# Where the weight conversion of the expert next but one stands among full and half slots, in attention with a mixture of experts

## The chip, the cores and the metric

One core of a Trainium2 chip runs the whole program. The metric is the device time of one execution in microseconds (us), and the time of a kernel is the median of its runs. A separate profiled execution gives the trace, on which all positions in time below ("at 395.56") are counted from the start of its span.

## What is computed

An attention step over 4 x 8 x 576 rows of 64 gives x, 2304 tokens of 512 numbers. Each token then goes to the one expert of eight with the largest logit, and is scaled by its softmax value:

```
logits = x @ w_gate                       # 2304 x 8
expert_idx = argmax(logits, axis=1)
gate_w = softmax(logits)[arange(N), expert_idx]
for e in range(8):
    xe = x[expert_idx == e]
    h = maximum(xe @ w1[e], 0.0)          # 512 -> 1024
    out[expert_idx == e] = gate_w[...] * (h @ w2[e])   # 1024 -> 512
```

Everything is float32 outside. How many tokens an expert has is known only on the chip, so the loops over the experts run on counts that are read from memory there.

## The kernel before

**Slots.** Attention and routing take the first 262 us or so; what follows is the experts. The kernel takes them in the order 1, 2, ... 7, 0, one position e = 0 to 7 after another ("the fourth expert" is e = 3). The tokens of an expert are cut into slots: full ones of 128 tokens, and behind them at most one half slot, for a rest of at most 64 tokens. A slot runs like this:

- GpSimd gathers the rows of 128 tokens for a later slot (L1489, with the copy of the indices in L1538) and scatters finished rows (L1504).
- VectorE splits the gathered rows into two f16 parts, `xn` (L1780, L1783).
- SP issues two transposing DMAs of `xn` into `xB` (`xtrans`, L1411). SP's queue also issues the weight loads (`load`, L1384), and takes both in program order.
- VectorE copies `xB` to `xT` (L1794), once both transposes have landed and TensorE no longer reads the old `xT`.
- TensorE runs the first product (`first_part`, L1582: 96 matmuls, 5.52 us in a full slot), VectorE applies the relu and splits the result (L1751, L1753), and TensorE runs the second product (`second_part`, L1598 in full and L1595 in half slots). ScalarE moves the result out (L1711 in full slots).

So the body of a slot on VectorE (`dve_body`, L1772) is: `xn` for the *next* slot, the two relus of this one, `xT` for the next one, and at the end the register loads for the next expert's counts (L1303).

**Weights.** The matmuls are f16, on weights that have been split into a high part (`conv_hi`, ScalarE, L1272) and a low part (`conv_lo`, VectorE, L1276). An expert's weights are eight units of 128 x 1024; four units are a "state". State i is a half of the weights of position 1 + i // 2, so the states 2e and 2e + 1 belong to the expert that follows e, and 2e + 2 and 2e + 3 to the one next but one. Loaded units lie in one of two staging buffers by the position's parity (`m_stage` or `mem` in the trace), converted ones in one of three (`m_w` and two named `mem`).

**Which slot converts what** is set by counters, on ScalarE and VectorE alike (`conv_loops`, L1319). For each e, whatever of `now` (2e, 2e + 1) is missing is converted in a first slot. Then `full(nxt)` (L1356) gives the full slots one state each of `nxt` (2e + 2, 2e + 3); and if there is a half slot, `last(nxt)` (L1365) looks whether a state of `nxt` is still missing, and converts it there. All these cases are written out one behind another in the program, and the counts choose among them by branches; so much of the code is jumped over.

**What SP loads when** follows a counter `ld` of the states loaded (L1430 to L1480). `turn(i)` stands for a slot that converts state i, `rest()` for a slot that converts nothing; each first issues the slot's transposes (`slot()`) and then loads one state ahead. A state's loads are four DMAs of 512 KB, and wait where the staging buffer is still to be converted.

The cut of the conversions in a slot's body (`K["cuts"]`, L1789) puts the four `conv_lo` of a full slot around the relus, one, one, and two behind the copy of `xT`; in a half slot all four stand behind that copy.

Of the kernel before, what the change touches and what calls it, by code (L numbers as in the profile page):

```python
# [1224 lines left out]
def experts(nc, tc, es, x_dram, mem, rout, w1, w2, out):  # L1225
# [16 lines left out]
    PE, A, V, G, SP = nc.tensor, nc.scalar, nc.vector, nc.gpsimd, nc.sync  # L1242
# [12 lines left out]
    with tc.tile_critical():  # L1255
# [63 lines left out]
        def conv_loops(eng, rr, body):  # L1319
# [11 lines left out]
            for e in range(NE):  # L1331
# [33 lines left out]
                def last(states):  # L1365
                    if states:
                        with eng.If(eng.snap(c) < states[0] + 1):
                            step(e, 1, states[:1])
                        with eng.Else():
                            last(states[1:])  # L1370
                    else:
                        step(e, 1)

                full(nxt)
                if nxt:
                    with eng.If(more[1]()):
                        last(nxt)
                else:
                    with eng.While(more[1]):
                        step(e, 1)  # L1380
# [7 lines left out]
        r2 = SP.alloc_register("m_sp_r2")  # L1388
        SP.reg_mov(r2, 2)
        splim = [SP.alloc_register(f"m_sp_lim{i}") for i in range(2)]  # L1390
        nt = {}
        for n in "hl":
            nt[n] = SP.alloc_register(f"m_sp_{n}")
# [33 lines left out]
        SP.wait_ge(S["cn"], 7)  # L1427
        SP.reg_mov(splim[1], 1)
        SP.reg_load(splim[0], cnt[0:1, 0, 1:2])
        for e in range(NE):  # L1430
            now, nxt = ([i for i in range(2 * e + k, 2 * e + k + 2) if c0 <= i < 14] for k in (0, 2))

            def more(r=r1):
                return SP.snap(r) < SP.snap(splim[e % 2])

            def slot():
                xtrans()
                if e + 1 < NE:
                    SP.reg_load(splim[(e + 1) % 2], cnt[0:1, e + 1, 1:2])

            def load_next(j):
                loads(j)
                SP.reg_mov(ld, j + 1)

            def turn(i):
                slot()
                if i == c0:
                    SP.wait_ge(S["sc0"], 16)
                    SP.sem_inc(S["ya"], 1)
                SP.reg_add(cr, cr, 1)  # L1450
                with SP.If(SP.snap(ld) < i + 1):
                    load_next(i)
                with SP.If(SP.snap(ld) < i + 2):
                    load_next(i + 1)
                with SP.Else():
                    load_next(i + 2)

            def rest():
                slot()
                if 2 * e + 5 < 14:  # L1460
                    with SP.If(SP.snap(ld) < 2 * e + 6):
                        load_next(2 * e + 5)

            def turns(states):
                if states:
                    with SP.If(more()):
                        turn(states[0])
                        turns(states[1:])
                else:
                    with SP.While(more):  # L1470
                        rest()

            if now:
                with SP.If(SP.snap(cr) < 2 * e + 2):
                    if len(now) == 2:
                        with SP.If(SP.snap(cr) < 2 * e + 1):
                            with SP.If(more(r2)):
                                turn(now[0])
                            with SP.Else():
                                turn(now[0])  # L1480
                                SP.reg_add(cr, cr, 1)
                    with SP.If(SP.snap(cr) < 2 * e + 2):
                        turn(now[-1])
            turns(nxt)
        for n in "hl":
            spw("tx" + n, nt[n])

# [354 lines left out]
```

## Time and profile before

| | us |
|---|---|
| median of 3 runs | 498.99 (498.46 to 499.39) |
| the profiled execution | 493.86 |
| its span in the trace | 492.1 |
| TensorE busy | 459.1 |
| VectorE busy | 355.0 |
| ScalarE busy | 221.3 |
| GpSimd busy | 213.4 |

The span is what the trace covers; the profiled execution lasted 1.8 us longer than that, and stands 5.1 us below the median of the runs. "Issue" in the rows is time in which an engine waited for nothing that the profile shows. A row of a timeline gives the start, the busy time, the engine, the line, what is written from what, the shape, the number of instructions in the row, and in brackets the idle time ahead of it with what ended it. PE is TensorE, DVE is VectorE, ACT is ScalarE, POOL is GpSimd; SPq is the time in which SP issues DMAs.

In this run the slots by position are: e = 0 three full ones (and one taken ahead of the loops), e = 1 one full, e = 2 seven full, e = 3 one half, e = 4 five full and a half, e = 5 one half, e = 6 a full and a half, e = 7 one half.

### The profile page before, as it was taken

Reading aid. Unit: us, or ns where it says so; the run is one execution under the profiler, and the core shown is the slowest. Engines: PE = TensorE matmul, PEld = TensorE weight load, DVE = VectorE, ACT = ScalarE, POOL = GpSimd, SP = SyncE. Lnnn points to the kernel's source line nnn. Section 1 sums busy time; section 2 is a strip of 40 time slices with the busy share of each in tenths; the row PEclk is TensorE's granted clock in tenths of the full one; section 3 lists DMA queues with packets and bytes.
Section 4 is the critical chain, followed back from the end, with each engine's and each line's share of the span. In section 5 each row is a group of like instructions: output and inputs, shape, how many; then the busy total and the mean of one; then the engine's idle time right before and its main releaser. Section 6 shows DMA issues by size and latency. Waiting matters only on the chain.

```text
span 492.1 us, 14309 instructions
## 1 busy us (share of the span) xinstructions
PE 459.1 (93%) x5279; PEld 314.1 (64%) x5280; DVE 355.0 (72%) x785; ACT 221.3 (45%) x361; POOL 213.4 (43%) x396
## 2 busy tenths in 40 slices
PE   2999899999999989999978999999999989999885
PEld 1555456666666646657656777676677767777864
DVE  2788489786869647989885778788843489844682
ACT  3788565556666655457610444433300163300701
POOL 6567657367748344656331423132232122232132
PEclk9999799999999999999989999999999999999999
DMA  5667979999899989885247999799973199963232
GB/s 119 137 119 158 182 158 172 174 193 228 175 161 164 272 164 191 183 177 209 65 135 286 253 332 254 231 261 305 274 182 98 45 256 304 318 139 90 57 73 69
DMA packets 170106, 90.57 MB, mean 184 GB/s; under 512 B 151471, under 2 KB 152751, under 8 KB 170032
## 3 DMA queue, kind: packets, MB, share of 16 engines
q1 hardware_dynamic: 166192, 77.95, 67.8%
q0 software_dynamic: 3840, 11.80, 7.8%
q8 instruction: 26, 0.43, 0.3%
q14 instruction: 48, 0.39, 0.3%
HBM read 55.35 MB, written 11.60 MB: 136 GB/s over the span
## 4 chain that ended last, share of the span: by engine, by line
PE 64%; DVE 12%; SPq 8%; DMA 6%; issue 5%; ACT 2%; POOL 1%; DVEq 1%; POOLq 0%; ACTq 0%
PE m_ph L1582 18%; PE m_py L1598 16%; PE o L565 7%; PE st L491 5%; SPq L275 3%; PE loc L677 3%; PE sm L596 3%; PE sn L404 2%; SPq L277 2%; DMA m_xB<-m_xn 2%; DMA QT<-mem 1%; DVE mem L1276 1%; PE wm L882 1%; DVE m_w L1276 1%; PE sn L421 1%
## 5 line engine op out<-in xcount | busy, mean ns | idle before, releaser
L1582 PEld LDWEIGHTS m_ph<-m_xT,mem 128*128 128x128 f16 x1344 | 66.0, 98 | 5.9 <-issue 3.3
L1582 PE MATMUL m_ph<-m_xT,mem 128*128 128x128 f16 (+1 forms) x1344 | 67.1, 212 | 2.6 <-DVE m_xT L1794 2.6
L1711 ACT ACTIVATE m_y<-m_py 128x512 f32<-128x512 f32 x17 | 10.2, 597 | 121.6 <-PE m_py L1598 121.6
L510 ACT ACTIVATE aT<-st 128x512 f32<-128x512 f32 x96 | 55.2, 594 | 17.6 <-PE st L491 17.1
L412 DVE TENSOR_REDUCE mt<-sn 128x1 f32<-128x512 f32 (+4 forms) x83 | 54.2, 663 | 12.2 <-PE sn L410 10.0
L495 POOL TENSOR_SCALAR_AFFINE_SELECT aT<-aT 128x128 f32<-128x128 f32 (+2 forms) x160 | 48.0, 317 | 31.9 <-ACT aT L510 29.9
L1598 PE MATMUL m_py<-mem,m_hT 128*128 128x512 f16 x264 | 58.9, 379 | 1.8 <-DVE m_hT L1751 1.8
L565 PE MATMUL o<-aT,mem 128*64 128x320 f32 (+4 forms) x320 | 59.2, 433 | 0.0
L1751 DVE TENSOR_SCALAR m_hT<-m_ph 128x512 f16<-128x512 f32 (+1 forms) x46 | 29.0, 631 | 38.5 <-PE m_ph L1582 37.3
L1538 POOL COPY m_ig<-r_idx 128x1 int32 x22 | 4.0, 184 | 112.9 <-DVE m_xn L1783 111.8
L491 PE MATMUL st<-mem 128*128 128x64 f16 (+6 forms) x224 | 46.8, 262 | 0.4 <-ACT aL L532 0.2
L1598 PEld LDWEIGHTS m_py<-mem,m_hT 128*128 128x128 f16 x264 | 25.3, 98 | 30.3 <-issue 2.0
L491 PEld LDWEIGHTS <-mem 128*128 128x128 f16 (+1 forms) x448 | 32.9, 99 | 16.3 <-issue 4.4
L1582 PEld LDWEIGHTS m_ph<-m_xT,m_w 128*128 128x128 f16 x768 | 40.9, 98 | 3.1 <-issue 1.1
L491 PE MATMUL st<-QT,mem 66*128 66x64 f16 (+6 forms) x224 | 42.3, 262 | 0.4 <-ACT QT L455 0.4
L1582 PE MATMUL m_ph<-m_xT,m_w 128*128 128x128 f16 (+1 forms) x768 | 41.8, 216 | 0.9 <-issue 0.7
L1598 PE MATMUL m_py<-m_w,m_hT 128*128 128x512 f16 x168 | 37.4, 379 | 0.0
L565 PEld LDWEIGHTS o<-aT,mem 128*64 128x64 f32 x320 | 25.3, 137 | 16.7 <-issue 9.8
L1504 POOL DMA_INDIRECT out_dram<-m_y,m_is x23 | 27.2, 1184 | 19.9 <-POOL m_is L1510 19.9
L404 PE MATMUL sn<-mem 128*128 128x128 f16 (+3 forms) x158 | 31.2, 275 | 1.5 <-DVE mt L412 1.1
L1490 POOL DMA_INDIRECT m_xg<-x_scratch,m_ig x22 | 24.0, 1089 | 17.5 <-POOL m_ig L1538 17.5
L1753 DVE SCALAR_TENSOR_TENSOR m_hT<-m_ph,m_hT 128x512 f16<-128x512 f32 (+1 forms) x46 | 29.1, 633 | 1.6
(259 smaller groups left out, 904.2 us busy)
## 6 DMA issues: line engine op xcount, KB each, us to landing
mem<-in_moe_w_dram SPq DMA_DIRECT2D x40, 512.0 KB, 6.1
m_stage<-in_moe_w_dram SPq DMA_DIRECT2D x24, 512.0 KB, 6.6
mem<-in_k_dram SPq DMA_DIRECT2D x32, 128.0 KB, 3.0
mem<-in_q_dram SPq DMA_DIRECT2D x32, 128.0 KB, 2.8
mem<-in_v_dram SPq DMA_DIRECT2D x32, 128.0 KB, 2.8
x_scratch<-xb SPq DMA_DIRECT2D x3, 1152.0 KB, 5.9
mem<-mem SPq DMA_DIRECT2D x6, 288.0 KB, 4.1
x_scratch<-xb SPq DMA_DIRECT2D x1, 864.0 KB, 3.8
```

The lines of the kernel that those rows point to most:

```text
L404: nc.tensor.matmul(ps[:, c:c + k1 - k0], QT[:, 5 * hh + t, :], keys(hh)[:, k0:k1], start=(c == 0), stop=(k1 == parts[-1][3] and hh == part ...
L412: nc.vector.reduce_max(out, v, axis=AX.X)
L491: nc.tensor.matmul(ps[:, c:c + n], kk[:, kb, :], qq[:, w:w + n], start=(first and i == 0 and j == 0), stop=(last and i == 1 and j == len(p ...
L495: nc.gpsimd.affine_select(out=ap, in_=ap, pattern=pattern, compare_op=ALU.is_ge, fill=0.0, base=base, channel_multiplier=-1)
L510: nc.scalar.activation(out=a, in_=ps, func=AF.Exp, scale=ESC)
L565: nc.tensor.matmul(o[64 * hh:64 * hh + 64, q0:q0 + n], vv, aa, start=(j == 0), stop=(j == 4), skip_group_check=True)
L1490: G.indirect_dma_start(out=x.rearrange("p h e -> p (h e)"), out_offset=None, in_=x_dram, in_offset=bass.IndirectOffsetOnAxis(ap=i, axis=0) ...
L1504: G.indirect_dma_start(out=out, out_offset=bass.IndirectOffsetOnAxis(ap=i, axis=0), in_=ysb[:, j], in_offset=None, bounds_check=bound, oob ...
L1582: mm = PE.matmul(ph[i2][:, f, 0:N], w[:, kc, c:c + 128], x[:, j, kc, 0:N], start=(i == 0), stop=(i == 11), skip_group_check=True)
L1598: mm = PE.matmul(py, hh, ww[:, 4 + ff // 2, c:c + 512], start=st, stop=sp_)
L1751: V.tensor_scalar(out=hT[i2][0][:, :, 0:N], in0=ph[i2][:, :, 0:N], scalar1=0.0, scalar2=None, op0=ALU.max).then_inc(S[hi], 1)
L1753: V.scalar_tensor_tensor(out=hT[i2][1][:, :, 0:N], in0=ph[i2][:, :, 0:N], scalar=0.0, in1=hT[i2][0][:, :, 0:N], op0=ALU.max, op1=ALU.subtr ...
```

## The change

On ScalarE and VectorE, `last` is given no states for e up to 4: a half slot of these experts converts nothing of the expert next but one. For e = 5 (the sixth position; later ones have no `nxt`) it is as before. On SP, `turns` follows: for e up to 4 only full slots make a `turn`, by a count of full slots that SP now loads for each expert (`spful`), and the half slot is a `rest()`. `rest()` now loads the states 2e + 4 and 2e + 5, whichever are not yet loaded, where it loaded 2e + 5 alone; and `turn` asks before it loads state i + 2. The new lines shift the numbers behind them by 2 to 10.

```diff
@@ -1374,7 +1374,7 @@
                 full(nxt)
                 if nxt:
                     with eng.If(more[1]()):
-                        last(nxt)
+                        last(nxt if e > 4 else [])
                 else:
                     with eng.While(more[1]):
                         step(e, 1)
@@ -1388,6 +1388,8 @@
         r2 = SP.alloc_register("m_sp_r2")
         SP.reg_mov(r2, 2)
         splim = [SP.alloc_register(f"m_sp_lim{i}") for i in range(2)]
+        spful = [SP.alloc_register(f"m_sp_ful{i}") for i in range(2)]
+        SP.reg_mov(spful[1], 1)
         nt = {}
         for n in "hl":
             nt[n] = SP.alloc_register(f"m_sp_{n}")
@@ -1427,6 +1429,7 @@
         SP.wait_ge(S["cn"], 7)
         SP.reg_mov(splim[1], 1)
         SP.reg_load(splim[0], cnt[0:1, 0, 1:2])
+        SP.reg_load(spful[0], cnt[0:1, 0, 0:1])
         for e in range(NE):
             now, nxt = ([i for i in range(2 * e + k, 2 * e + k + 2) if c0 <= i < 14] for k in (0, 2))
 
@@ -1437,6 +1440,8 @@
                 xtrans()
                 if e + 1 < NE:
                     SP.reg_load(splim[(e + 1) % 2], cnt[0:1, e + 1, 1:2])
+                    if e + 1 < 5:
+                        SP.reg_load(spful[(e + 1) % 2], cnt[0:1, e + 1, 0:1])
 
             def load_next(j):
                 loads(j)
@@ -1453,17 +1458,19 @@
                 with SP.If(SP.snap(ld) < i + 2):
                     load_next(i + 1)
                 with SP.Else():
-                    load_next(i + 2)
+                    with SP.If(SP.snap(ld) < i + 3):
+                        load_next(i + 2)
 
             def rest():
                 slot()
-                if 2 * e + 5 < 14:
-                    with SP.If(SP.snap(ld) < 2 * e + 6):
-                        load_next(2 * e + 5)
+                for j in (2 * e + 4, 2 * e + 5):
+                    if j < 14:
+                        with SP.If(SP.snap(ld) < j + 1):
+                            load_next(j)
 
             def turns(states):
                 if states:
-                    with SP.If(more()):
+                    with SP.If(more() if e > 4 else SP.snap(r1) < SP.snap(spful[e % 2])):
                         turn(states[0])
                         turns(states[1:])
                 else:
@@ -1482,6 +1489,9 @@
                     with SP.If(SP.snap(cr) < 2 * e + 2):
                         turn(now[-1])
             turns(nxt)
+            if nxt and e < 5:
+                with SP.If(more()):
+                    rest()
         for n in "hl":
             spw("tx" + n, nt[n])
 
```

VectorE at the end of the half slot of e = 3, before: behind the copy of `xT` come four conversions (`m_w_4100` is a converted unit, `mem_61` a staged one), then the counts and the jump to the next expert.

```order
L1753 SCALAR_TENSOR_TENSOR m_hT_4112<-m_ph_4123,m_hT_4111 128x4x64
L1794 COPY m_xT<-m_xB 128x1024
L1276 SCALAR_TENSOR_TENSOR m_w_4100<-mem_61,m_w_4100 128x1024 x4
L1303 TENSOR_LOAD r_cnt x2
L1310 ISA
L1367 UNCONDITIONAL_BRANCH
```

The same place after:

```order
L1763 SCALAR_TENSOR_TENSOR m_hT_4112<-m_ph_4123,m_hT_4111 128x4x64
L1804 COPY m_xT<-m_xB 128x1024
L1303 TENSOR_LOAD r_cnt x2
L1310 ISA
L1376 UNCONDITIONAL_BRANCH
L1335 COMPARE_AND_BRANCH
```

The conversions are gone from this branch; the copy is followed by the counts.

SP in the half slot of e = 3, before (`m_stage_4113` takes the units of states 10 and 11, `mem_61` those of 8 and 9): behind the two transposes stand three loads of a state under branches, of which the counter lets one run.

```order
L1411 DMA_TRANSPOSE m_xB<-m_xn_4106 128x4x128
L1439 TENSOR_LOAD r_cnt
L1450 ISA
L1451 COMPARE_AND_BRANCH
L1384 DMA mem_61<-in_moe_w_dram 128x1024 x4
L1451 UNCONDITIONAL_BRANCH
L1453 COMPARE_AND_BRANCH
L1384 DMA mem_61<-in_moe_w_dram 128x2x512 x4
L1453 UNCONDITIONAL_BRANCH
L1384 DMA m_stage_4113<-in_moe_w_dram 128x1024 x4
```

The same slot after:

```order
L1413 DMA_TRANSPOSE m_xB<-m_xn_4106 128x4x128
L1442 TENSOR_LOAD r_cnt
L1444 TENSOR_LOAD r_cnt
L1468 COMPARE_AND_BRANCH
L1384 DMA m_stage_4113<-in_moe_w_dram 128x1024 x4
L1468 UNCONDITIONAL_BRANCH
L1468 COMPARE_AND_BRANCH
L1384 DMA m_stage_4113<-in_moe_w_dram 128x2x512 x4
L1468 UNCONDITIONAL_BRANCH
```

Here the loads of states 10 and 11 stand one behind the other, each under its own branch, and a second register load has come in.

## Rows read from the trace of the kernel before

**Rows 1.** The page, busy time of each engine, share of the span, instructions.
```profile
PE 459.1 (93%) x5279; PEld 314.1 (64%) x5280; DVE 355.0 (72%) x785; ACT 221.3 (45%) x361; POOL 213.4 (43%) x396
```

**Rows 2.** Timeline, ScalarE: start, busy, line, out<-in, [idle before <-releaser].
```profile
392.90 3.90 ACT L1272 ACTIVATE m_w<-mem 128x1024 f16<-128x1024 f32 x4 [3.31 <-issue]
```

**Rows 3.** Timeline, VectorE, around the fourth expert's half slot (e = 3).
```profile
389.54 0.49 DVE L1780 TENSOR_SCALAR m_xn<-m_xg 128x512 f16<-128x512 f32 x1 [4.10 <-issue]
...
394.77 0.64 DVE L1794 COPY m_xT<-m_xB 128x1024 f16<-128x1024 f16 x1 [2.23 <-DMA m_xB<-m_xn]
395.33 4.61 DVE L1276 SCALAR_TENSOR_TENSOR m_w<-mem,m_w 128x1024 f16<-128x1024 f32 x4
399.87 0.47 DVE L1780 TENSOR_SCALAR m_xn<-m_xg 128x512 f16<-128x512 f32 x1
...
401.12 0.68 DVE L1751 TENSOR_SCALAR m_hT<-m_ph 128x512 f16<-128x512 f32 x1
```

**Rows 4.** Timeline, TensorE, first two full slots of e = 4.
```profile
395.56 5.52 PE L1582 MATMUL m_ph<-m_xT,mem 128*128 128x128 f16 x96 [1.09 <-DVE m_xT L1794]
...
401.95 5.34 PE L1598 MATMUL m_py<-mem,m_hT 128*128 128x512 f16 x24 [0.87 <-DVE m_hT L1751]
407.13 5.52 PE L1582 MATMUL m_ph<-m_xT,mem 128*128 128x128 f16 x96
...
417.67 5.52 PE L1582 MATMUL m_ph<-m_xT,mem 128*128 128x128 f16 x96
```

**Rows 5.** Chain of waits: start, length, what; ahead of fourth and sixth expert.
```profile
386.74 2.39 issue
...
454.35 0.14 issue
```

**Rows 6.** Timelines of VectorE and TensorE, into the sixth expert (e = 5).
```profile
453.09 0.42 DVE L1794 COPY m_xT<-m_xB 128x1024 f16<-128x1024 f16 x1
...
454.90 0.49 DVE L1780 TENSOR_SCALAR m_xn<-m_xg 128x512 f16<-128x512 f32 x1 [1.39 <-issue]
...
461.72 0.43 DVE L1794 COPY m_xT<-m_xB 128x1024 f16<-128x1024 f16 x1 [2.81 <-DMA m_xB<-m_xn]
...
462.29 5.52 PE L1582 MATMUL m_ph<-m_xT,mem 128*128 128x128 f16 x96 [1.16 <-DVE m_xT L1794]
```

**Rows 7.** Timeline of SP's DMA queue: start of issue, time issuing, line, DMAs.
```profile
260.31 4.03 SPq L1384 DMA_DIRECT2D mem<-in_moe_w_dram  x8
...
390.23 2.57 SPq L1411 DMA_TRANSPOSE m_xB<-m_xn  x2
394.26 2.41 SPq L1384 DMA_DIRECT2D m_stage<-in_moe_w_dram  x4
400.56 2.64 SPq L1411 DMA_TRANSPOSE m_xB<-m_xn  x2
404.56 1.95 SPq L1384 DMA_DIRECT2D m_stage<-in_moe_w_dram  x4
409.34 2.61 SPq L1411 DMA_TRANSPOSE m_xB<-m_xn  x2
```

**Rows 8.** DMA traffic in 40 equal slices: 260 to 278, then 404 to 416 us.
```profile
GB/s 0 0 46 200 328 400 337 382 391 377 308 363 366 397 428 391 432 378 406 413 388 381 410 364 373 387 401 387 387 396 354 275 102 22 101 343 437 0 0 0
...
GB/s 239 61 169 384 258 41 130 273 369 314 328 205 116 246 225 212 348 362 342 300 355 396 396 410 403 437 370 379 329 223 155 58 164 365 161 15 68 352 307 423
```

**Rows 9.** Timeline, VectorE: the copy for the slot from 417.67.
```profile
415.74 0.43 DVE L1794 COPY m_xT<-m_xB 128x1024 f16<-128x1024 f16 x1 [0.51 <-DMA m_xB<-m_xn]
```

**Rows 10.** Stretches: us, busy PE PEld DVE ACT POOL, granted clock, DMA share, GB/s.
```profile
261.30:268.30 7.00, 7.00 (x98) 5.70 (x96) 3.60 (x7) 0.00 (x0) 1.51 (x3) 1.00 0.99 366
405.60:413.40 7.80, 7.80 (x109) 6.48 (x108) 7.48 (x10) 4.50 (x5) 1.66 (x3) 1.00 1.04 295
251.40:254.70 3.30, 1.20 (x16) 0.79 (x15) 3.21 (x15) 0.84 (x2) 1.30 (x3) 1.00 0.50 171
254.80:258.10 3.30, 3.30 (x27) 2.09 (x26) 2.21 (x12) 0.80 (x4) 0.00 (x0) 0.50 0.43 112
```

## The prediction

> **What bounds the kernel now.** I read the page first: TensorE is busy for 459.1 us, 93% of the span [rows 1], so an edit counts only where TensorE stands idle, or where it would come to stand. The edit acts on slots with at most 64 tokens. The trace shows the order of the slots by the moving columns of L1582: after seven full slots comes one half slot (the fourth expert, e = 3), then five full slots and a half slot (e = 4), a half slot (e = 5), a full and a half slot (e = 6) and a half slot (e = 7); the first three experts have no half slot. In before, the half slot of e = 3 converts four units (ACT L1272, 3.90 us; VectorE L1276, 4.61 us for four) [rows 2, 3], the half slot of e = 4 converts nothing because everything up to state 11 is done by then, and that of e = 5 is the one the edit exempts. So in this run the edit acts in one place: state 8 goes from the half slot of e = 3 to the first full slot of e = 4, and states 9, 10 and 11 each go one full slot later.
>
> So I read the timeline around 395 us. TensorE ends the half slot, waits 1.09 us for VectorE's copy of xT, runs L1582 of the first full slot of e = 4 at 395.56, waits 0.87 us for VectorE's L1751, and starts the second full slot at 407.13 [rows 4]. From 395.56 to 407.13 are 11.57 us; the next slot takes 10.54 us, from 407.13 to 417.67 [rows 4]. VectorE shows why: its four L1276 occupy 395.33 to 399.94, and only behind them come the xn of the next slot (399.87) and the L1751 for which TensorE waits (401.12) [rows 3]. The first wait is another matter: xT is copied at 394.77, when the transposes have landed, and these start behind the xn of 389.54, ahead of which VectorE stood 4.10 us in "issue" [rows 3]. The chain of waits puts 2.39 us of it behind a single branch, at 386.74 [rows 5].
>
> **The change, part by part.**
>
> *Removed from the half slot:* four L1276, 4.61 us of VectorE, and four L1272 on ACT. Without them xn follows its xT copy as at the end of the next half slot, where no conversion stands between: copy 453.09, xn 454.90 [rows 6], 1.81 us. So xn comes at 394.77 + 1.81 = 396.6 instead of 399.87, the L1751 is ready when L1582 is, and the slot takes 10.54 instead of 11.57 us: **-1.03 us**. The wait of 1.09 us stays, as nothing in front of 389.54 gets shorter on that path.
>
> *Added to the four full slots of e = 4:* one conversion each in slots one to four instead of one to three. That costs nothing: the slot from 407.13 holds a conversion on both engines and takes 10.54 us [rows 4]. The cover is TensorE's own time; four L1276 are 4.61 us of it.
>
> *Moved on SP, the term that decides.* The queue of SP issues both the weight loads and the transposes that xT waits for, in program order. In before the half slot of e = 3 issues four loads at 394.26 (state 10), then come the next slot's transposes at 400.56, and state 11's four loads only behind these, at 404.56 [rows 7]. In after, rest() issues the loads of states 10 and 11 together in the half slot: eight DMAs of 512 KB, and the next slot's transposes stand behind all eight. Issuing eight took 4.03 us at 260.31 [rows 7], so SP is free at 394.26 + 4.03 = 398.3, early enough for transposes that in before start at 400.56. But the data are not there: in the stretch that begins with the eight loads of 260.31 the traffic stays between 300 and 432 GB/s until the slice at 273.95 and falls to 102 and 22 GB/s behind it, at 274.4 [rows 8], 14.1 us after the first issue. The same from 394.26 gives 408.4 for the drain.
>
> Do the transposes pass the loads? Two rows say no. With four loads issued at 404.56, the transposes are issued at 409.34 [rows 7]; the loads drain at about 413.3 (40 slices of 0.3 us from 404: 223, 155, 58 GB/s in the 30th to 32nd) [rows 8], and xT is copied at 415.74, after a DMA wait of 0.51 us [rows 9], 2.4 us after the drain and 6.4 us after the issue. With no load in flight the same transposes went from issue at 390.23 to the copy at 394.77 in 4.54 us [rows 3, 7]. So xT of the second full slot is copied at 408.4 + 2.4 = 410.8, and TensorE starts 395.56 - 394.77 = 0.8 us later, at 411.6, instead of 407.13: **+4.5 us**, the first gain already inside. The bounds: the loads, one gather (128 rows of 2304 B) and half a scatter are about 4.6 MB; at the 366 and 295 GB/s of two stretches full of loads [rows 10], counted from about 395.3, they drain at 407.9 and 410.9, and with 1.5 to 2.4 us to the copy TensorE starts at 410.2 to 414.1: +3.1 to +7.0 us. I take 4.5, since the stretch at 260 us is the same eight loads.
>
> The Trainium skill speaks to this as well: "DMA: Bandwidth & Descriptors", section "Queues, rings and completion order", has each DMA engine consume the descriptors of one issuing queue in ring order, which is against this change, and the row at 415.74 agrees. Its section "Specifications" gives 435 GB/s as the ceiling; by that alone 4.6 MB would drain in an estimated 10.6 us, TensorE would start near 409.1, and the term would be +2.0; the 295 to 366 GB/s of this trace decide.
>
> *TensorE's clock.* TensorE then stands idle from 395.56 + 10.54 = 406.1 to 411.6, 5.5 us, longer than the idle rows of TensorE quoted here (1.16 us at most) [rows 6]. After sparse work the granted clock has fallen to 0.50, the 1.2 GHz level: with TensorE busy for 1.20 of 3.30 us ahead of it, the stretch 254.80 to 258.10 ran at 0.50 [rows 10]. At half the clock 3.4 us of stretch do 1.7 us of work. I take one such stretch, **+1.7 us**, between 0 (it falls and recovers while TensorE is idle) and 3.4 (two of them).
>
> *The rest costs nothing.* SP's extra register load per slot falls into its wait for xn: xn starts at 399.87, and SP issues the transposes only at 400.56 [rows 3, 7]; uncovered it would be an estimated few tenths of a us per slot, since the whole time from the end of that xn at 400.34 to the issue is 0.22 us. States 12 and 13 are loaded in the third and fourth full slot of e = 4, one later than before; the conversion of state 12 stands in the half slot of e = 5, behind the copy at 461.72 [rows 6], some 30 us later. They meet the transposes as the loads at 404.56 do, and these delayed no matmul: xT copied at 415.74, next slot at 417.67.
>
> **Sum:** 4.5 + 1.7 = +6.2 us. The profiled execution lasted 493.86 us, and this sum would make it 500.1; the median of the runs is 498.99, 5.1 us above it, and I add the difference to the median: **505.2 us**.
>
> **The rivals.**
>
> *A code fetch falls on the chain of the sixth expert.* VectorE's program is shorter by the conversions of five experts. The chain shows the same jump over untaken code twice: at 386.74, ahead of the fourth expert, it waits 2.39 us, and at 454.35, ahead of the sixth, 0.14 us [rows 5]. The second stands directly ahead of the xn at 454.90, from which transposes and the copy at 461.72 follow, for which TensorE waits 1.16 us [rows 6]; there a wait of 2.39 instead of 0.14 passes on in full: +2.25, 507.5 us. For it: which pair waits can only depend on where the code lies, and all code behind the first expert moves. Against: in before one of the two waits. The mirror case, that the wait at 386.74 goes and none comes, moves everything behind 389.54 forward by 2.25: 503.0 us. The Trainium skill has the mechanism in "Runtime: NRT & Kernel Launch", section "Instruction fetch mechanics": a taken branch that leaves the two pages at hand waits for a DMA fetch; no row here shows pages.
>
> *The transposes are not held up.* Then the slot starts when TensorE is free, at 406.1, the clock stays up, and what is left is -1.03 us: 498.0. This decides itself at one point: xT must be copied by 405.3, so transposes must land some 5 us ahead of the 410.8 above. For it: transposes have been issued while loads were in flight in most slots, and in them TensorE ran on. Against: those had four loads ahead of them, not eight, and were issued 5 us behind the loads; and 4.6 MB by 404 would be over 500 GB/s, more than any stretch of [rows 8] or [rows 10].
>
> *The change does not do what it says,* because the slots are other ones than I read: time as before, 499.0.
>
> **How the numbers follow.** Transposes behind eight loads: 0.50, 502.0 to 509.4 (3.1 + 0 to 7.0 + 3.4 us); with the fetch at the sixth expert 0.28, at 507.5; with the wait at 386.74 gone 0.07, at 503.0; transposes not held 0.11, at 498.0, about two thirds of it beyond 0.2% (1.0 us, about what a measurement of this kernel can tell from no change); no effect 0.04. Slower 0.85, same 0.07, faster 0.08. The range 502.0 to 509.4 leaves out the last two and the upper end of the fetch case.
>
> **What would show it.** In the profile after: no L1276 between the xT copy near 394.8 and the next xn; eight L1384 in a row on SP ahead of a transpose; VectorE's copy of the following xT with a DMA wait of 4 us or more; a TensorE idle of some 5.5 us ahead of the second full slot of e = 4, and a stretch of clock 0.50 behind it; at the sixth expert an "issue" wait of over 2 us, or none. I am wrong if that copy waits under 1 us, and wrong in size if the traffic drains before 407 or the clock stays at 1.00.

## The result and the profile after

| | before | after |
|---|---|---|
| median of 16 runs each, us | 498.5 (495.14 to 502.3) | 504.85 (500.14 to 509.2) |
| ratio, 95% interval | | 1.012 (1.009 to 1.0149) |
| profiled execution, us | 493.86 | 504.78 |
| stretch of the experts in that trace, us | 226.34 | 235.02 |

The change makes the kernel slower, by 6.35 us between the medians and by 6.0 us (interval 4.5 to 7.4 us) by the ratio; 6.2 were forecast. Medians and ranges here and below are over all runs, while the ratios leave out single runs more than 1.5% above the fastest of their kernel (2 of 16 after the change, 5 of 12, at 502.8 to 506.5 us, of the kernel below that loads one state, at most 2 of any other, one of them at 915.81 us), and what made these longer is not shown. The profiled execution of before stood 4.6 us under its median, so the two traces must not be subtracted from end to end. I took a second trace of each kernel (told below), and compare by slots: from the first L1582 matmul (L1592 after the change) of one slot to that of the next, in TensorE's timeline. "Stretch of the experts" is from the first such matmul to the end of the last matmul. The slots that differ (the others sum to -0.28 us):

| us | before, two traces | after, two traces | mean difference |
|---|---|---|---|
| full slot of e = 1 and first of e = 2 | 22.26, 22.28 | 22.01, 21.31 | -0.61 |
| half slot of e = 3 | 6.90, 6.76 | 6.09, 6.08 | -0.75 |
| first full slot of e = 4 | 11.57, 11.57 | 16.59, 16.48 | +4.97 |
| second full slot of e = 4 | 10.54, 10.54 | 12.42, 12.76 | +2.05 |
| half slots of e = 4 and e = 5 | 13.00, 14.40 | 15.78, 15.71 | +2.05 |
| stretch of the experts | 226.34, 228.24 | 235.02, 234.42 | +7.43 |

The page's busy times after the change, answering to [rows 1]:

```profile
PE 462.4 (92%) x5279; PEld 316.5 (63%) x5280; DVE 355.7 (71%) x785; ACT 221.4 (44%) x361; POOL 214.7 (43%) x396
```

VectorE's and ScalarE's work is the same; TensorE's is 3.3 us longer for the same 5279 matmuls; 2.2 us of this lie in the stretch of the experts, and the clock explains most of these below. TensorE's timeline, answering to [rows 4]:

```profile
390.31 2.96 PE L1592 MATMUL m_ph<-m_xT,mem 128*128 128x64 f16 x96
...
396.40 5.54 PE L1592 MATMUL m_ph<-m_xT,mem 128*128 128x128 f16 x96
401.77 5.34 PE L1608 MATMUL m_py<-mem,m_hT 128*128 128x512 f16 x24
412.99 7.40 PE L1592 MATMUL m_ph<-m_xT,mem 128*128 128x128 f16 x96 [5.88 <-DVE m_xT L1804]
420.23 5.34 PE L1608 MATMUL m_py<-mem,m_hT 128*128 128x512 f16 x24
```

The waits for VectorE's L1751 and for the first copy of xT are gone; in their place stands one wait of 5.88 us for the copy that opens the second full slot of e = 4, and the 96 matmuls behind it take 7.40 us where they took 5.52. VectorE in the same place, its timeline, answering to [rows 3]:

```profile
395.24 0.46 DVE L1804 COPY m_xT<-m_xB 128x1024 f16<-128x1024 f16 x1 [1.04 <-DMA m_xB<-m_xn]
396.90 0.49 DVE L1790 TENSOR_SCALAR m_xn<-m_xg 128x512 f16<-128x512 f32 x1 [1.21 <-DMA m_xg<-x_scratch,m_ig]
...
412.42 0.43 DVE L1804 COPY m_xT<-m_xB 128x1024 f16<-128x1024 f16 x1 [7.90 <-DMA m_xB<-m_xn]
```

No L1276 stands between the first copy and xn, so xn comes 1.66 us behind its copy (5.10 before). The next copy then waits 7.90 us for its transposes. SP's queue, answering to [rows 7], and two pieces of the chain of waits (start, length, what) with the issue of the first transpose and the wait for both (the row of four transposes also holds the two of the slot behind):

```profile
394.97 6.32 SPq L1384 DMA_DIRECT2D m_stage<-in_moe_w_dram  x8
402.81 15.49 SPq L1413 DMA_TRANSPOSE m_xB<-m_xn  x4
```

```profile
402.81 1.96 SPq L1413
...
404.97 7.35 DMA m_xB<-m_xn
```

Eight loads go out together, over 6.32 us. In the DMA view of two stretches (packets, MB, and how many are small: the transposes' packets have 256 B, and some of 4 and 8 B also count as small) one sees what passes when; the first line is 403 to 408 us, the second 408 to 412.5:

```profile
DMA packets 963, 2.00 MB, mean 399 GB/s; under 512 B 129, under 2 KB 129, under 8 KB 962
```

```profile
DMA packets 1422, 0.90 MB, mean 200 GB/s; under 512 B 1114, under 2 KB 1114, under 8 KB 1421
```

All 129 small packets of the first line are of 4 or 8 B, so no packet of the transposes passes while the loads fill the engines, though the first transpose was issued from 402.81 to 404.77 and the second from 404.97 on; all 1024 of the two are in the second line, from 408.9 on, and the copy follows at 412.42. The clock, in the view by stretches (busy times as in [rows 10], then the granted clock, DMA share, GB/s), ahead of the second full slot and in it:

```profile
407.10:412.90 5.80, 0.01 (x1) 0.00 (x0) 0.48 (x2) 4.49 (x5) 0.00 (x0) 0.76 0.95 217
410.20:413.00 2.80, 0.01 (x1) 0.04 (x2) 0.58 (x2) 1.96 (x3) 0.00 (x0) 0.50 0.53 68
413.00:416.40 3.40, 3.40 (x33) 3.40 (x34) 3.26 (x4) 0.00 (x0) 0.00 (x0) 0.50 0.00 0
416.40:420.40 4.00, 4.00 (x67) 3.93 (x65) 2.51 (x3) 0.00 (x0) 2.21 (x4) 0.93 0.60 126
```

The granted clock falls while TensorE is still idle, at about 410.1, and stays at 0.50 until about 417.0 (worked out from the 0.93 of the last line), so some 4.0 us of it fall on matmuls: in the first 3.4 us 33 of them start, where at full clock some 59 do (96 in 5.52 us). 0.50 is the 1.2 GHz level. And at the sixth expert the chain of waits has, where [rows 5] had 0.14 us:

```profile
463.09 2.28 issue
```

### The profile page after: what moved, and what is told of

Read it like the earlier page. It is cut to its first block, busy times and chain, and to the rows that moved or that the text cites. A ratio compares the mean times of both kernels' runs of the same rounds, so it can differ in the third digit from the quotient of the medians.

```text
span 502.7 us, 14361 instructions
## 1 busy us (share of the span) xinstructions
PE 462.4 (92%) x5279; PEld 316.5 (63%) x5280; DVE 355.7 (71%) x785; ACT 221.4 (44%) x361; POOL 214.7 (43%) x396
## 4 chain that ended last, share of the span: by engine, by line
PE 63%; DVE 11%; DMA 9%; SPq 7%; issue 5%; ACT 2%; POOL 1%; DVEq 1%; POOLq 0%; ACTq 0%
PE m_ph L1592 18%; PE m_py L1608 15%; PE o L565 7%; PE st L491 6%; PE sm L596 3%; DMA QT<-mem 2%; SPq L275 2%; DMA m_xB<-m_xn 2%; PE loc L677 2%; PE sn L404 2%; SPq L277 1%; DMA mem<-mem 1%; DVE mt L412 1%; SPq L1384 1%; SPq L1413 1%
## 5 line engine op out<-in xcount | busy, mean ns | idle before, releaser
L1592 PE MATMUL m_ph<-m_xT,mem 128*128 128x128 f16 (+1 forms) x1344 | 69.1, 214 | 8.4 <-DVE m_xT L1804 8.3
L1592 PEld LDWEIGHTS m_ph<-m_xT,mem 128*128 128x128 f16 x1344 | 67.8, 99 | 12.1 <-issue 9.7
L1592 PEld LDWEIGHTS m_ph<-m_xT,m_w 128*128 128x128 f16 x768 | 41.0, 98 | 2.8 <-issue 1.1
L1592 PE MATMUL m_ph<-m_xT,m_w 128*128 128x128 f16 (+1 forms) x768 | 41.8, 216 | 0.8 <-issue 0.8
L1514 POOL DMA_INDIRECT out_dram<-m_y,m_is x23 | 29.8, 1297 | 19.9 <-POOL m_is L1520 10.5
```

The costliest lines, as they stand in the source:

```text
L1514: G.indirect_dma_start(out=out, out_offset=bass.IndirectOffsetOnAxis(ap=i, axis=0), in_=ysb[:, j], in_offset=None, bounds_check=bound, oob ...
L1592: mm = PE.matmul(ph[i2][:, f, 0:N], w[:, kc, c:c + 128], x[:, j, kc, 0:N], start=(i == 0), stop=(i == 11), skip_group_check=True)
```

## The experiments

Theory: the eight loads ahead of the transposes make the loss, and the idle time that they cause brings the clock down; the moved conversions themselves gain about 1 us; the place of VectorE's code costs some 2 us at the sixth expert. Rivals: the moved conversions cost; the traffic, and not its order in SP's queue, holds the transposes; the code's place makes the whole of what the loads don't. The ratios are to the kernel before on the same chip, with 95% intervals; "after" stands at 1.012.

| kernel | median, us | ratio | half slot e = 3 | first full, e = 4 | second full | half slots of e = 4 and 5 |
|---|---|---|---|---|---|---|
| half slot loads one state | 499.29 | 0.9976 (0.9934 to 1.0019) | 5.97 | 12.39 | 10.54 | 13.97 |
| before, eight loads | 505.27 | 1.0136 (1.0090 to 1.0182) | 6.78 | 17.68 | 12.35 | 14.00 |
| after, code kept | 504.3 | 1.0093 (1.0055 to 1.0131) | 7.37 | 17.33 | 12.99 | 12.21 |
| before, conversions moved | 499.93 | 0.9996 (0.9959 to 1.0034) | 7.19 | 11.55 | 10.54 | 12.27 |
| four loads on ScalarE's queue | 507.91 | 1.0244 (1.0193 to 1.0296) | 6.04 | 18.34 | 12.81 | 15.91 |
| six loads | 503.77 | 1.0122 (1.0084 to 1.0159) | 6.02 | 14.32 | 13.16 | 16.03 |
| no loads, code kept | 495.68 | 0.9952 (0.9917 to 0.9987) | 7.56 | 10.54 | 10.54 | 12.77 |
| no loads, code of after | 496.89 | 0.9944 (0.9912 to 0.9977) | 6.10 | 10.55 | 10.54 | 14.50 |
| eight loads in a full slot | 501.41 | 1.0039 (0.9997 to 1.0080) | 7.15 | 10.54 | 12.78 | 12.20 |

(For the last one the third full slot takes 12.16 us; in all the others it takes 10.54.)

**One state in the half slot.** The changed kernel with this edit:

```diff
             if nxt and e < 5:
                 with SP.If(more()):
-                    rest()
+                    rest((2 * e + 4,))
```

(`rest` takes the states as an argument.)

> The changed kernel, but its half slots of the first five experts load one state (four DMAs) instead of two; state 11's loads then stand behind the next slot's transposes, as before the change. If the eight loads ahead of the transposes are what costs, the copy of xT for the second full slot of e = 4 waits under 1 us for its DMA instead of 7.9 us, TensorE starts that slot with no idle time, the granted clock stays at 1.00 there, and the time falls by about 7 us from 504.8 to about 498; the issue wait of 2.28 us ahead of the sixth expert stays, so it ends nearer 499 than 497.5. If moving the conversions is what costs, or the traffic itself and not its order, the time stays at 504 to 505.

499.29 us in the median (493.63 to 506.51), near what was expected: the ratio shows no loss, and in the trace (of an execution of 495.26 us) the clock stays up. But the copy did not come at once. VectorE's copy and TensorE's second full slot, from their timelines:

```profile
406.22 0.43 DVE L1804 COPY m_xT<-m_xB 128x1024 f16<-128x1024 f16 x1 [3.70 <-DMA m_xB<-m_xn]
...
406.79 5.52 PE L1592 MATMUL m_ph<-m_xT,mem 128*128 128x128 f16 x96 [1.68 <-DVE m_xT L1804]
```

It waits 3.70 us, not under 1, and the slot ahead of it takes 12.39 us, not 10.54. So four loads hold the transposes too. The stretch behind ran at full clock:

```profile
406.80:410.20 3.40, 3.40 (x62) 3.40 (x63) 3.29 (x5) 3.37 (x4) 0.00 (x0) 1.00 0.00 0
```

**The eight loads alone.** The kernel before, with state 11 loaded behind state 10 in the half slot:

```diff
                 with SP.Else():
-                    load_next(i + 2)
+                    with SP.If(SP.snap(ld) < i + 3):
+                        load_next(i + 2)
+                    if i == 8:
+                        load_next(i + 3)
```

> The kernel before, all conversions where they were, but the half slot of e = 3 loads states 10 and 11 together. If the eight loads are what costs, the second full slot of e = 4 starts some 5 us later than in the kernel before, a stretch at clock 0.50 follows (+1.9 us), and the time is about 505 (498.5 + 6.9). If it takes the moved conversions to make the loss, the time stays at 498.5. No wait of over 2 us ahead of the sixth expert, since VectorE's code is that of before.

505.27 us, all of the loss without moving one conversion. TensorE's timeline:

```profile
420.25 7.33 PE L1585 MATMUL m_ph<-m_xT,mem 128*128 128x128 f16 x96 [5.95 <-DVE m_xT L1797]
```

The wait of 5.95 us and the matmuls of 7.33 us are much like the 5.88 and 7.40 of the changed kernel. The two slots around it take 24.46 us, 1.8 more than there.

**The code kept.** The changed kernel, with the half slots' conversions in the program but never run:

```diff
-                        with eng.If(eng.snap(c) < states[0] + 1):
+                        with eng.If(eng.snap(c) < (states[0] + 1 if e > 4 else 1)):
...
-                        last(nxt if e > 4 else [])
+                        last(nxt)
```

> The changed kernel, but ScalarE and VectorE keep the code of the half slots' conversions, under a condition that is never true, so that the code lies where it lay before. If the wait of 2.28 us ahead of the sixth expert is a matter of where the code lies, it shrinks to the 0.14 us of before, TensorE's wait in front of the seventh expert's first slot falls from 2.14 to about 1.2 us, and the time falls by about 2.2 us to 502.6; the 5.9 us idle of TensorE at the second full slot of e = 4 stays. If the wait belongs to the moved work, it stays, and so does 504.8.

The wait depends on where the code lies (that it is a fetch of code is not shown): xn of the sixth expert's slot has 1.40 us of "issue" ahead of it here, 3.55 in the changed kernel. VectorE's timelines of this kernel and of the changed one:

```profile
468.81 0.49 DVE L1790 TENSOR_SCALAR m_xn<-m_xg 128x512 f16<-128x512 f32 x1 [1.40 <-issue]
```

```profile
465.77 0.49 DVE L1790 TENSOR_SCALAR m_xn<-m_xg 128x512 f16<-128x512 f32 x1 [3.55 <-issue]
```

But the total is 504.3 and not 502.6, a miss: what the two half slots of e = 4 and 5 gain (12.21 for 15.78 us) is lost elsewhere; the half slot of e = 3 takes 7.37 for 6.09 us, and the first slots of e = 1 and 2 take 25.21 for 22.01. Of the latter some 1.7 us are the clock and not the code: behind an idle time of 2.05 us in the first slot of e = 2 the granted clock was 0.64 over the next 3.4 us, and these 24 matmuls took 7.03 us where they take 5.34 elsewhere:

```profile
323.46 7.03 PE L1608 MATMUL m_py<-m_w,m_hT 128*128 128x512 f16 x24 [2.05 <-DVE m_hT L1761]
```

**The conversions alone.** The kernel before with the first of these two lines:

```diff
-                        with eng.If(eng.snap(c) < states[0] + 1):
+                        with eng.If(eng.snap(c) < (states[0] + 1 if e > 4 else 1)):
```

> The kernel before with the conversions alone moved: the half slots of the first five experts convert nothing, by a condition that is never true, SP's part and the code's place as before. If the prediction's first term is right, the second full slot of e = 4 follows the first after 10.5 instead of 11.6 us, VectorE's L1276 is gone behind the xT copy at about 394.8, and the time is about 1 us below the kernel before: 497.5. If the conversions cost as much in the full slots as they cost in the half slot, the time is 498.5; if they delay TensorE there, more.

499.93 us, ratio 0.9996: no gain that can be measured, where 1 us was expected, and the first full slot takes 11.55 us, as before. VectorE and TensorE, timelines:

```profile
400.15 0.49 DVE L1780 TENSOR_SCALAR m_xn<-m_xg 128x512 f16<-128x512 f32 x1 [0.94 <-DMA m_xg<-x_scratch,m_ig]
...
410.34 0.43 DVE L1794 COPY m_xT<-m_xB 128x1024 f16<-128x1024 f16 x1 [2.88 <-DMA m_xB<-m_xn]
...
410.91 5.52 PE L1582 MATMUL m_ph<-m_xT,mem 128*128 128x128 f16 x96 [0.86 <-DVE m_xT L1794]
```

xn starts 0.79 us into the slot (399.36) instead of 4.31, and the wait for L1751 is gone. The transposes only go out sooner into the four loads, and a wait of 0.86 us for xT has taken the place of the 0.87 us. So the conversions in the half slot had cost nothing, since the transposes behind the loads would have been as late.

**Order or traffic.** Four of the eight loads on another queue:

```diff
                     with eng.If(more[1]()):
                         last(nxt if e > 4 else [])
+                        if e == 3 and eng is A:
+                            for e2, u in half_of(11):
+                                A.wait_ge(S["clo"], 16 + split(e2 - 2, u))
+                                A.dma_start(out=as_unit(stage[e2 % 2][u], u), ...)
```

(SP's half slot loads state 10 alone.)

> The changed kernel, but in the half slot of e = 3 SP loads state 10 alone, and ScalarE issues the four loads of state 11 on its own queue at the end of that slot, some 3 us after SP's four: the same bytes at about the same time, but only four loads ahead of the transposes in SP's queue. If the order in SP's queue is what holds the transposes, the half slot and the first full slot of e = 4 take about 18.5 us together, as with one state loaded (18.36), against 22.68 in the changed kernel, the copy of xT waits about 4 us for its DMA, and the time is about 499.5. If it is the traffic that holds them, whichever queue it is on, the two slots take about 22.7 us, the copy waits about 8 us, and the time is 504.8.

My theory failed this one: 24.38 us for the two slots, and 507.91 us. The timelines of ScalarE's queue, of SP's (transposes of three slots in one row, the first issued at 397.24) and of VectorE, and the DMA queues from 407 to 413 us (packets, MB, share of the engines' time; q10 is ScalarE's queue, q1 SP's, which by then holds the transposes):

```profile
396.76 0.44 ACTq L1381 DMA_DIRECT2D m_stage<-in_moe_w_dram  x1
...
397.25 2.48 ACTq L1381 DMA_DIRECT2D m_stage<-in_moe_w_dram  x3
```

```profile
397.24 33.04 SPq L1417 DMA_TRANSPOSE m_xB<-m_xn  x6
```

```profile
413.56 0.43 DVE L1810 COPY m_xT<-m_xB 128x1024 f16<-128x1024 f16 x1 [8.48 <-DMA m_xB<-m_xn]
```

```profile
q10 hardware_dynamic: 706, 1.35, 75.6%
q1 hardware_dynamic: 904, 0.22, 18.6%
```

Both queues move packets through nearly the whole stretch, 706 and 904 (840 of these are the transposes' 256 B), but the loads' are some eight times as large (1.35 MB against 0.22), and the transposes end with the loads. So it doesn't free the transposes that half of the loads are in another queue: they share the 16 engines with what is in flight there. (Transposes in a queue without any loads of its own were not tried.) Nor is it the late issue that holds them: in the changed kernel SP came to the first transpose at 402.81, here at 397.24, and they land no sooner (copies at 412.42 and 413.56); in the two traces of the changed kernel the eight loads took 6.32 and 4.72 us to issue, and the copy came 17.45 and 17.34 us after the first of them. The Trainium skill bears on this in "DMA: Bandwidth & Descriptors", section "Queues, rings and completion order": an engine takes turns between the queues that have work for it; the two counts above agree. The Trainium skill's other rule there, ring order within a queue, fits the changed kernel, where none of the transposes' packets passed while the loads filled the engines (403 to 408 us) and all 1024 after 408.9.

**Six loads.** State 10 and half of state 11 in the half slot, the other half in the next slot:

```diff
+                    if e == 3:
+                        for x in half_of(11)[:2]:
+                            load(*x)
+                        SP.reg_mov(ld, 12)
```

> The changed kernel, but the half slot of e = 3 loads six units, state 10 and half of state 11; the other two come behind the next slot's transposes. From four to eight loads the two slots around it grew from 18.36 to 22.68 us, 1.1 us for each load; if each load ahead of the transposes costs the same, they take about 20.5 us here, TensorE idles for 3.5 to 4 us ahead of the second full slot of e = 4. If the clock falls after any idle time of some us, the following slot takes about 12.4 us as with eight loads and the time is 502.5; if 3.5 us of idle time don't bring it down, that slot takes 10.54 us, and the time is 500.7.

The two slots take 20.34 us, in step with 18.36 for four loads and 22.56 to 22.68 for eight: 1.0 to 1.1 us for each load. With the code of before each load costs more, 1.5 us: 24.46 us (the eight loads alone) and 24.70 (the code kept) for eight, 18.40 (the mean of before) and 18.74 (the conversions alone) for four; why is not shown. The clock fell all the same. TensorE's timeline and two stretches:

```profile
413.74 8.14 PE L1599 MATMUL m_ph<-m_xT,mem 128*128 128x128 f16 x96 [3.61 <-DVE m_xT L1811]
```

```profile
410.10:413.70 3.60, 0.03 (x1) 0.00 (x0) 0.53 (x2) 3.01 (x4) 0.00 (x0) 0.83 1.24 245
413.70:417.10 3.40, 3.36 (x32) 3.39 (x33) 3.29 (x4) 1.48 (x2) 0.00 (x0) 0.50 0.46 169
```

Behind an idle time of 3.61 us the slot took 2.62 us longer than at full clock, no less than behind the 5.88 and 5.76 us of the changed kernel (1.88 and 2.22). What differs is how much of the slow stretch falls on matmuls: here the clock is at 0.50 for 5.5 us from the start of the slot (413.70 to 419.20), there for some 4.0 and 4.7 us. The time is 503.77, above the 502.5 expected for this case.

**No loads in the half slot.** The conversions moved, the code kept, and:

```diff
                 SP.reg_add(cr, cr, 1)
+                if e == 3 and i == 8:
+                    return
```

> The kernel with the conversions alone moved (code place as before), and SP's half slot of e = 3 loads nothing; states 10 and 11 are loaded in the first and second full slot of e = 4, behind the transposes. If four loads ahead of the transposes were already what kept the first full slot at 11.55 us when the conversions had gone, it takes 10.54 us here, the copy of xT waits for no DMA, and the time is about 1 us below the kernel with the conversions alone moved, some 0.5 to 1.5 us below the kernel before: 497.5. If something else held that slot, it stays at 11.5 us, and the time at 498.5 to 500.

```profile
406.16 0.42 DVE L1796 COPY m_xT<-m_xB 128x1024 f16<-128x1024 f16 x1
...
408.68 5.52 PE L1584 MATMUL m_ph<-m_xT,mem 128*128 128x128 f16 x96
```

Now the copy waits for nothing, the slot takes 10.54 us, and the kernel is faster than before: 495.68 us, ratio 0.9952 (0.9917 to 0.9987). With the kernel that moves the conversions alone this shows that four loads ahead of the transposes already held that slot.

**The kernel before, again.**

> The kernel before once more, for a second trace. The first trace stood 5 us below the median. If its stretch of the experts (226.3 us from the first to the last matmul of the slots) was as long as in other executions, it comes out within 1 us of that; if the waits for code fell luckily there, it comes out 1 to 3 us longer, above all in the first slots of e = 1 and e = 2 (22.26 us) and in the half slot of e = 3 (6.90 us).

499.51 us, and 228.24 us of experts, 1.9 more than in the first trace; not in the places that I named, but in the half slots of e = 4 and 5 (14.40 for 13.00) and in the first slot (11.37 for 10.99). Why these slots were shorter in the first trace is not shown.

**Eight loads in a full slot.** The kernel without loads in the half slot, with states 10 and 11 together in the first full slot of e = 4:

```diff
-                if e == 3 and i == 8:
+                if (e, i) in ((3, 8), (4, 10)):
                     return
...
+                if (e, i) == (4, 9):
+                    load_next(11)
```

> The kernel whose half slot of e = 3 loads nothing (code place of before), but with states 10 and 11 loaded together in the first full slot of e = 4, behind the transposes for the second, and none in the second. In the changed kernel the copy of xT came 17.45 us after the first of eight loads was issued. Counted from the load that stands at 403.65 us in the kernel without loads in the half slot, the copy would come at 421.1 instead of 416.70, some 2.4 us after TensorE wants it. So if eight loads cost what a slot cannot hide of 17.45 us, the second full slot takes about 13 us instead of 10.54, the loss is 2 to 3 us (about 498) against 5 to 6 in the half slot, and it shows whether 2.4 us of idle time bring the clock down. If the half slot alone is where such loads cost, every full slot takes 10.54 us and the time is 495.7.

```profile
404.56 4.37 SPq L1384 DMA_DIRECT2D m_stage<-in_moe_w_dram  x8
...
422.16 0.43 DVE L1798 COPY m_xT<-m_xB 128x1024 f16<-128x1024 f16 x1 [4.10 <-DMA m_xB<-m_xn]
...
422.74 7.15 PE L1586 MATMUL m_ph<-m_xT,mem 128*128 128x128 f16 x96 [2.08 <-DVE m_xT L1798]
```

The copy comes 17.60 us after the first load was issued (17.45 and 17.34 in the changed kernel, 18.49 and 18.47 in the two kernels with eight loads and the code of before), and the slot takes 12.78 us, as expected. The half slot is not special; what matters is how much of these 17.3 to 18.5 us passes before TensorE wants the copy. The clock fell here after only 2.08 us of idle time, and the slot behind took 12.16 us; so the price on TensorE was 2.24 + 1.62 = 3.9 us and not 2.4, and the time 501.41 us, where some 498 had been expected:

```profile
422.70:426.10 3.40, 3.37 (x39) 3.40 (x40) 3.29 (x4) 3.12 (x4) 0.00 (x0) 0.63 0.00 0
```

But 2.08 us is no threshold. In the second trace of the kernel before TensorE stood idle for longer ahead of the full slot of e = 6, and the clock stayed at 1.00 (96 matmuls in 5.52 us):

```profile
467.05 5.52 PE L1582 MATMUL m_ph<-m_xT,mem 128*128 128x128 f16 x96 [2.40 <-DVE m_xT L1794]
```

The same holds in that place for 2.14 and 2.09 us in the two traces of the changed kernel. So for idle times of some 2.0 to 2.4 us the length alone doesn't decide.

**No loads, the code of after.** The changed kernel with

```diff
-                    rest()
+                    rest(() if e == 3 else (2 * e + 4,))
```

> The changed kernel, its code without the half slots' conversions, but the half slot of e = 3 loads nothing. It differs from the kernel with no loads there and the code kept only in where the code lies. If that place costs at the sixth expert (an issue wait of 3.55 us ahead of xn instead of 1.40) and gains at e = 1 to 2, as in the traces so far (half slots of e = 4 and 5 together 15.4 against 13.1 us on average, the full slot of e = 1 and the first of e = 2 together 22.4 against 23.0), it is about 1.6 us slower: 497.3. The first full slot of e = 4 takes 10.54 us in both. If the place of the code costs nothing in sum, both take the same, 495.7.

496.89 us and a ratio of 0.9944, against 0.9952 with the code kept: no difference that can be measured, where I expected 1.6 us. The slots show one reason. The place of the code costs 1.73 us at the sixth expert (14.50 for 12.77 us; "issue" ahead of xn 3.75 for 1.40) and gives back 1.46 us at the fourth (half slot 6.10 for 7.56):

```profile
460.36 0.49 DVE L1790 TENSOR_SCALAR m_xn<-m_xg 128x512 f16<-128x512 f32 x1 [3.75 <-issue]
```

```profile
456.82 0.49 DVE L1782 TENSOR_SCALAR m_xn<-m_xg 128x512 f16<-128x512 f32 x1 [1.40 <-issue]
```

In the six traces with the shorter code that half slot takes 5.97 to 6.10 us, in the seven with the code of before 6.76 to 7.56.

**The changed kernel, again.**

> The changed kernel once more, for a second trace. The stretch of the experts took 226.34 and 228.24 us in the two traces of the kernel before, and 235.02 in the one of the changed kernel. If the loss is made at the fourth expert's half slot and the slots behind it, the half slot and first full slot take 22.5 to 24.5 us, the second full slot 12 to 13 us, the half slots of e = 4 and 5 together 15 to 16 us, and the stretch 233 to 236 us.

503.89 us and 234.42 us of experts. The slots stand in the table of the result, all inside the bounds named, the first pair at their lower end (22.56 us).

## Why the prediction was right, and where it was not

The time was forecast as 505.2 and came out at 504.85, a loss of 6.35 against 6.2 us. Step by step:

*The place.* The edit acts in one place, as said: the half slot of e = 3 and the slots behind it. What else moved is put down to where the code lies; the runs show this for the half slot of e = 3 and for the sixth expert.

*The gain of 1.03 us* was the step that failed. I took the wait for L1751 as the only thing between 11.57 and 10.54 us. The kernel with the conversions alone moved shows 11.55: the transposes would have been late in any case, since four loads stood ahead of them. The wait of 1.09 us ahead of that slot, which I had kept, went too, but by the code's place: the half slot takes 5.97 to 6.10 us in all six traces with the shorter code. I had asked of each stall what is late next only for the eight loads, not for the four of before. The gain is real only without any loads there (10.54 us, and 0.5% of the kernel's time). It did not spoil the sum, because the +4.5 us had been worked out from the drain of the loads and didn't rest on it.

*Transposes behind eight loads, +4.5 us net.* Right in kind, shown by the eight loads alone (+1.36%) and by four in their place (0.9976). In size: the half slot and the first full slot together grew by 4.22 us (22.62 for 18.40, means of two traces each). The copy was forecast for 410.8 and came at 412.42, in a trace that stood 0.84 us later at 396.40. SP spent 6.32 us on the eight issues (4.72 in the second trace), not the 4.03 of [rows 7], without effect on the copy, and the transposes' packets passed from 408.9 on, close to the drain forecast at 408.4.

*Why they wait* was only half right. I put it down to the order of one queue. Within SP's queue the packets do go in order; but with half of the loads on a second queue they share the engines with these and end no sooner (24.38 us). What counted here is the bytes in flight, and not the order of one queue alone.

*The clock, +1.7 us.* Right, and a little small: 1.88 and 2.22 us in the two traces. I took 3.4 us of matmuls at 0.50, and in the first trace it was some 4.0, the rest of a stretch of some 6.9 us that had begun while TensorE was idle. The term doesn't grow with the idle time: behind 3.61 us of it the slot took 2.62 us longer, behind 2.08 us 1.62, and behind 1.68 us no longer; nor did one behind 2.40 us in the second trace of before. What else decides is open.

*The fetch at the sixth expert* was a rival with 0.28, and it came: 2.28 us of "issue" at 463.09, forecast 2.39. The two half slots there take 2.05 us longer. But it does not pass on in full, as I had it: with the same wait (2.28 us in the chain) the kernel that loads one state takes 13.97 us there, less than the 14.40 of the second trace of before, which hasn't got it. And the total didn't rise to 507.5: the same shortening of the code gave back 0.75 us at the half slot of e = 3, and the start of e = 2 was 0.61 us shorter, by what isn't shown. I had priced one jump of a program whose jumps all move; the two kernels without loads, which otherwise differ only in SP's branches and register loads, measure the same.

*Sum.* The slots give 7.43 us between the means of two traces each, the runs 6.35 with an interval of 4.5 to 7.4; I don't know what of the difference is chance. The two terms of the forecast are right for their slots, 4.22 + 2.05 = 6.27 us against 6.2, but some of that is luck: the first full slot alone grew by 4.97, and 0.75 was taken off by the shorter half slot, which I had at nothing. The other rivals fell: transposes that are not held, no effect, and the wait at 386.74 gone (in its place stand 1.97 us, at 388.41).

## What to carry to other kernels

Transfers on the critical path are held by the bulk loads in flight: here by those ahead of them in their own queue, and no less when half of the loads came through another. So issue bulk loads behind them, and in the slot with the most time; each 512 KB load too many cost 1.0 to 1.5 us of delay here. Before taking credit for a stall that goes, ask what is late next, also for the work of the kernel before. Where code is jumped over, an edit that shortens it can move the wait of every jump: price the sum of them, or measure it with the old code kept but never run.

## What the runs showed of the hardware

- Transposes of 256 B packets beside four loads on a second queue ended no sooner than behind eight on their own: 706 packets of the loads' queue and 904 of the transposes' in the same 6 us, 75.6% and 18.6% of the engines' time, and the copy 18.99 us after the first load (17.34 to 18.49 behind eight).
- The granted clock was 0.63 over the 3.4 us behind an idle time of 2.08 us and 0.64 behind one of 2.05, but stayed at 1.00 behind others of 2.09, 2.14 and 2.40 us. An idle time of 3.61 us cost no less than one of 5.88 (2.62 and 1.88 us), as more of the slow stretch fell on matmuls.
- The issue of eight loads by SP took 4.03 us in the kernel before (at 260.31), 4.37 with eight loads in a full slot, and 6.32 and 4.72 us in the half slot of the two traces of the changed kernel. Why is not shown.
- VectorE's wait behind a jump over untaken code came and went with the place of the code: 3.53 to 3.75 us of "issue" ahead of xn at the sixth expert in the six traces with the shorter code, 1.39 to 1.43 in the seven with the code of before.
